# Other release and set points for loads and turns in a gated attention unit followed by an expert layer; one buffer moved from the gate tiles to the score tiles

## The chip, the cores and the metric

The kernel runs on one core of one Trainium2 chip. The metric is the device time of one execution in microseconds. Each version was run several times, in rounds with the kernel before on the same chip. Runs within 1.5% of the fastest of the same kernel count as fast, and only those are compared. A ratio is the mean time of one kernel's fast runs over that of the other's of the same rounds, so it is not quite the ratio of the medians quoted beside it.

## The reference

Per batch of 8, with 3008 rows: z is 64 wide, u and v are 256 wide.

```python
scores = (1 / S) * z @ z.T
attn   = maximum(scores, 0) ** 2
x      = u * (attn @ v)              # 24064 rows in all
h      = x @ w_in                    # 256 -> 2048
out    = (h * cos(h)) @ w_out        # 2048 -> 256
```

## The kernel before

A batch is cut into 6 chunks of 512 columns; a chunk is 8 steps of the schedule, a batch 48. `at(t, rank, f)` puts the emission of `f` at step t; all events are sorted by t and then emitted, so a set point largely decides the order of instructions on each engine. The scores are symmetric: a group (c, R) of four 128x512 score tiles is computed once and its mirror image is made by a DMA transpose, here called a turn. All turns stand on one queue, that of SyncE, nearly in the order of emission; the orders told below are read from the traces. Plain loads with a cast are issued by GpSimd (POOL in the profile).

```python
    def hold(dma):                       # a DMA waits for the last matmul emitted before it
        if before:
            after(dma.ins, before[-1], SYNC)

    def turn_z(b):                       # next batch's z, 13 + 12 blocks of 128x128
        for k in range(2):
            hold(nc.sync.dma_start_transpose(zT[b % 2][...], zst[...]))

    def s_diagonal(b, c, also):          # half of group (c, c), completed by three small turns
        ...
    def s_group(b, c, R, also=None):
        if R == c and not direct(b, c, R):
            return s_diagonal(b, c, also)
        ...                              # scores, relu (ACT), square (DVE) into tile `a`
        if R > c and not direct(b, R, c):
            nc.sync.dma_start_transpose(tt, t)        # the score turn

    for b in range(B):                   # t = 48 * b
        ...
            at(t - 3.5 * U, 0, lambda b=b: load_z(b))       # step -28 of the next batch
            at(t - 2.25 * U, 0, lambda b=b: turn_z(b))      # step -18
            for g in range(NG):                             # v loads at -20, -14, -8
                at(t + (0.75 * g - 2.5) * U, 0, lambda b=b, g=g: load_v(b, g))
        # (cuts; the first score group of a batch stands at step -13.1,
        #  groups (4,5) and (5,5) of the batch before at -18.1 and -17.1)
```

## Time and profile before

The median was 1270.74 us in the first rounds. The page's first part (share of the span in which each engine is busy) and its row of the granted TensorE clock (40 equal slices, tenths of full speed). PE is TensorE, PEld its weight loads, DVE VectorE, ACT ScalarE, POOL GpSimd, and SPq below is the queue of SyncE:

```profile
span 1270.7 us, 20219 instructions
PE 1249.6 (98%) x7533; PEld 673.1 (53%) x7533; DVE 787.8 (62%) x1302; ACT 854.4 (67%) x1516; POOL 145.8 (11%) x201
...
PEclk9989999999999999999999999999999999999999
```

TensorE bounds the kernel. The table of windows, one line per batch period (length, busy time of each engine, clock, DMA share, GB/s), shows that a batch in the middle has no idle TensorE at all:

```profile
207.56:363.53 155.97, 155.97 (x950) 84.77 (x948) 97.36 (x163) 107.67 (x192) 17.91 (x24) 1.00 0.74 118
```

Most of what is lost, about 17 of 21 us, is lost in the first 85 us. The list of waits of TensorE (total us, times, longest us), where `x` is VectorE's gating of a finished chunk and `a<-a` are the three turns of a diagonal group:

```profile
PE acc L308 <- DVE x L324: 7.9, 3, 5.4
PE acc L308 <- DMA a<-a: 2.4, 1, 2.4
...
PE acc L308 <- DMA v_0_65<-in_v_dram: 1.0, 1, 1.0
```

The timeline of SyncE's queue says why the gate of chunk 2 came 5.4 us late: its u turn stood behind five score turns that took 30.9 us.

```profile
34.92 30.91 SPq L268 DMA_TRANSPOSE tt<-a  x5
66.00 1.81 SPq L149 DMA_TRANSPOSE ut<-ust_61  x1
```

And the timeline around the end of a batch. Second column: duration; for the queue this is the time to issue, not to land.

```profile
250.76 4.57 SPq L112 DMA_TRANSPOSE zT_63<-zst  x2
...
255.43 3.65 SPq L268 DMA_TRANSPOSE tt<-a  x1
259.19 3.75 SPq L233 DMA_TRANSPOSE a<-a  x3
...
263.96 0.89 POOL L89 DMA_DIRECT2D v_1_66<-in_v_dram  x1 [10.38 <-PE w L338]
...
265.92 0.45 PE L218 MATMUL w<-zT_63 64*128 64x512 f16 x4
```

The next batch's z turns are issued at 250.8 us and used at 265.9 us, 15 us later.

### The profile page before, as it was taken

How to read it: one execution, taken by the hardware profiler on the slowest of the kernel's cores; microseconds unless marked ns; L12 is line 12 of the kernel's file. 1: busy time of each engine (PE TensorE's matmuls, PEld its weight loads, DVE VectorE, ACT ScalarE, POOL GpSimd, SP SyncE). 2: the span in 40 equal slices, each digit the busy share in tenths (PEclk: the TensorE clock that was granted, in tenths of full speed). 3: DMA queues.
4: the chain of work that ended last, by engine and by line, in shares of the span. 5: the costliest groups of instructions: out<-in, count | busy, mean ns of one | idle time of the engine just before them, and what ended most of it. 6: DMA issues, size and time to landing. Idle time of an engine off the chain costs nothing.

```text
span 1270.7 us, 20219 instructions
## 1 busy us (share of the span) xinstructions
PE 1249.6 (98%) x7533; PEld 673.1 (53%) x7533; DVE 787.8 (62%) x1302; ACT 854.4 (67%) x1516; POOL 145.8 (11%) x201
## 2 busy tenths in 40 slices
PE   8879999999999999999999999999999999999998
PEld 3335555555555555555555555555555555555556
DVE  6746666666666666665666666665666666665555
ACT  5646776666767666676667666766677666676646
POOL 3201101110011100211002110011100111000000
PEclk9989999999999999999999999999999999999999
DMA  9988855887679775888568885688857798565311
GB/s 157 149 142 129 136 103 94 125 119 137 100 110 125 127 113 106 118 133 123 101 109 111 136 139 91 106 115 138 126 93 118 109 144 115 107 109 100 76 34 43
DMA packets 485042, 145.03 MB, mean 114 GB/s; under 512 B 433232, under 2 KB 484944, under 8 KB 484944
## 3 DMA queue, kind: packets, MB, share of 16 engines
q1 hardware_dynamic: 357312, 88.92, 41.9%
q0 software_dynamic: 100400, 29.77, 24.3%
q10 hardware_dynamic: 27232, 25.06, 6.9%
q8 instruction: 59, 0.97, 0.3%
q14 instruction: 39, 0.32, 0.1%
HBM read 60.29 MB, written 24.64 MB: 67 GB/s over the span
## 4 chain that ended last, share of the span: by engine, by line
PE 96%; DMA 3%; DVE 1%; ACT 0%; SPq 0%; issue 0%; DVEq 0%
PE acc L308 36%; PE yp L362 26%; PE w L338 25%; PE w L248 5%; PE w L218 1%; DMA tt<-a 1%; DMA ut<-ust_62 1%; PE acc L281 1%; PE w L362 1%; DMA v_0_65<-in_v_dram 1%; DMA a<-a 0%; DMA ut<-ust_61 0%; PE w L453 0%; DVE g L345 0%; DVE x L324 0%; SPq L268 0%
## 5 line engine op out<-in xcount | busy, mean ns | idle before, releaser
L338 PE MATMUL w<-x,w_in_72 128*128 128x512 f16 x1504 | 447.0, 380 | 0.6 <-DVE g L345 0.3
L362 PE MATMUL yp<-w_out_73,g 128*128 128x256 f16 x2944 | 442.4, 273 | 0.4 <-ACT ob L370 0.4
L362 PEld LDWEIGHTS <-g 128*128 128x128 f16 x3008 | 285.2, 98 | 207.4 <-issue 41.5
L260 ACT ACTIVATE rt<-w 128x512 f16<-128x512 f32 x485 | 250.8, 602 | 110.9 <-PE w L248 110.9
L263 DVE TENSOR_TENSOR a<-rt 128x1024 f16<-128x1024 f16 x252 | 172.5, 690 | 158.9 <-ACT rt L260 156.0
L338 PEld LDWEIGHTS <-w_in_72 128*128 128x128 f16 x1504 | 147.2, 98 | 22.9 <-issue 4.2
L89 POOL DMA_DIRECT2D ust_62<-in_u_dram x64 | 45.2, 711 | 369.4 <-PE w L248 361.9
L228 ACT ACTIVATE rt<-w 128x512 f16<-128x512 f32 (+3 forms) x180 | 64.1, 442 | 32.6 <-PE w L218 32.6
L308 PE MATMUL acc<-a,v_2_70 128*128 128x512 f16 x304 | 76.1, 379 | 0.0
L308 PE MATMUL acc<-a,v_2_67 128*128 128x512 f16 x304 | 75.8, 379 | 0.0
L89 POOL DMA_DIRECT2D ust_61<-in_u_dram x48 | 36.1, 758 | 317.0 <-PE acc L308 304.5
L308 PE MATMUL acc<-tt,v_0_68 128*128 128x512 f16 (+1 forms) x288 | 70.3, 373 | 0.0
L324 DVE TENSOR_TENSOR x<-acc,ut 128x128 f16<-128x128 f32 (+7 forms) x89 | 62.5, 713 | 9.4 <-DMA ut<-ust_61 5.9
L229 DVE TENSOR_TENSOR a<-rt 128x512 f16<-128x512 f16 (+3 forms) x180 | 49.3, 323 | 30.6 <-ACT rt L228 27.8
L308 PE MATMUL acc<-a,v_1_66 128*128 128x512 f16 x224 | 57.7, 387 | 9.5 <-DVE x L324 7.1
L308 PEld LDWEIGHTS <-v_1_66 128*128 128x128 f16 x384 | 36.7, 98 | 57.3 <-issue 17.2
L308 PE MATMUL acc<-tt,v_0_65 128*128 128x512 f16 (+1 forms) x264 | 64.3, 373 | 0.0
L308 PEld LDWEIGHTS <-v_0_65 128*128 128x128 f16 x384 | 36.8, 98 | 50.0 <-issue 7.6
L308 PEld LDWEIGHTS <-v_0_68 128*128 128x128 f16 x384 | 36.9, 98 | 45.8 <-issue 3.4
L308 PEld LDWEIGHTS <-v_1_69 128*128 128x128 f16 x384 | 36.9, 98 | 45.0 <-issue 2.6
L370 ACT ACTIVATE ob<-yp 128x512 f32<-128x512 f32 x92 | 55.8, 607 | 1.2 <-PE yp L362 1.2
L308 PE MATMUL acc<-a,v_1_69 128*128 128x512 f16 x224 | 56.2, 379 | 0.0
(1557 smaller groups left out, 1501.2 us busy)
## 6 DMA issues: line engine op xcount, KB each, us to landing
out_dram<-ob ACTq DMA_DIRECT2D x94, 256.0 KB, 3.1
ust_61<-in_u_dram POOLq DMA_DIRECT2D x48, 128.0 KB, 5.8
ust_62<-in_u_dram POOLq DMA_DIRECT2D x32, 128.0 KB, 3.4
a<-a SPq DMA_TRANSPOSE x135, 2.9
v_0_65<-in_v_dram POOLq DMA_DIRECT2D x4, 512.0 KB, 6.7
v_1_66<-in_v_dram POOLq DMA_DIRECT2D x4, 512.0 KB, 7.1
v_0_68<-in_v_dram POOLq DMA_DIRECT2D x4, 512.0 KB, 7.3
v_1_69<-in_v_dram POOLq DMA_DIRECT2D x4, 512.0 KB, 6.5
```

The costliest lines, as they stand in the source:

```text
L89: hold(nc.gpsimd.dma_start(dst, src))
L218: chain(nc.tensor.matmul(sps[k][:, k * P:], zt[h, j0 + k, :], zt[h, j0 + k:j0 + K, :].rearrange("p j w -> p (j w)"), start=True, stop=True))
L228: nc.scalar.activation(rt[:, i, k * P:], sps[k][:, k * P:], AF.Relu)
L229: nc.vector.tensor_tensor(t[:, k, k:, :].rearrange("p s w -> p (s w)"), rt[:, i, k * P:], rt[:, i, k * P:], ALU.mult)
L248: chain(nc.tensor.matmul(sps[k], zt[h, R * K + k + 1 - lo, :], zt[h, j0:j0 + K, :].rearrange("p j w -> p (j w)"), start=True, stop=True))
L260: nc.scalar.activation(rt[:, i, :], sps[k0 + i], AF.Relu)
L263: nc.vector.tensor_tensor(tv, rv, rv, ALU.mult)
L308: chain(nc.tensor.matmul(acc[:, nh, 0:wn], vt[:, j % G, nh * P:(nh + 1) * P], a, start=(n == 0), stop=(n == NJ - 2)))
L324: nc.vector.tensor_tensor(xs[m][:, :, at:at + n], acc[:, :, o:o + n], ut[:, :, o:o + n], ALU.mult)
L338: chain(nc.tensor.matmul(hp, w_in16[:, k, ft * P:(ft + 1) * P], x[:, k, :], start=(k == 0), stop=(k == NDH - 1)))
L362: chain(nc.tensor.matmul(ys[m][:, ts % YP, :], gs[(m, ft // FG)][:, ft % FG, ts * P:(ts + 1) * P], w_out16[:, ft, :], start=(n % (YP * NFT ...
L370: nc.scalar.activation(ob, ys[m], AF.Copy, bias=0.0, scale=inv_s2)
```

## The change

It tries to shorten the start (loads released earlier, the u turn of chunk 2 earlier on the queue, no turns for group (0,3,3), more `a` buffers), and to move the next batch's z load and z turns later.

```diff
-        if before:
-            after(dma.ins, before[-1], SYNC)
+        after(dma.ins, gate[0] if gate else before[-1], SYNC)   # gate: 5th of 8 warm-up matmuls
...
-    gpool = pool("g", 7)
+    gpool = pool("g", 6)
-    apool = pool("a", 8)
+    apool = pool("a", 9)
...
-        if R == c and not direct(b, c, R):
+        if R == c and (b, c) > (0, 3):          # (0,3,3) becomes a full group
...
-                at(12 + 3 * q, 0, lambda q=q: load_w_out(q))
+                at(15 + 2 * q, 0, lambda q=q: load_w_out(q))
...
-            at(t - 3.5 * U, 0, lambda b=b: load_z(b))
-            at(t - 2.25 * U, 0, lambda b=b: turn_z(b))
+            at(t - 2.75 * U, 0, lambda b=b: load_z(b))       # step -22
+            at(t - 2.125 * U, 0, lambda b=b: turn_z(b))      # step -17
...
-            at(t + c * U + (1 if c != 1 or b else -3), 0, lambda b=b, c=c: turn_u(b, c))
+            at(t + c * U + (1 if b or c not in (1, 2) else -3 * c), 0, lambda b=b, c=c: turn_u(b, c))
```

Between steps -18 and -17 stands the score group (5,5). The turn of (4,5), emitted at -18.1, stands in the trace before the change just behind the z turns of -18 (at 255.43 us). So on SyncE's queue the z turns fall from before the score turn of (4,5) to behind that turn and behind the three turns of (5,5).

More of the change, by code (lines that the diff above doesn't have):

```diff
@@ L81, in chain @@
         before.append(mm.ins)
+    gate = []
     def hold(dma):
-        if before:
-            after(dma.ins, before[-1], SYNC)
+        after(dma.ins, gate[0] if gate else before[-1], SYNC)
     def load(dst, src):
@@ L430 @@
                 at(-80 + i, 0, f)
+            at(-70, 0, gate.clear)
             at(2, 0, lambda: load_u(0, 2))
@@ L454, in prepare @@
                 wp, zero[:, 0, 0:P], zero[:, 0, :], start=True, stop=True))
+            if i == 4:
+                gate.append(before[-1])
         make_identity(nc, ident)
```

## The prediction

> **What bounds it.** TensorE is busy 98% of 1270.7 us (page, part 1); the table of windows by batch shows it busy 155.97 of 155.97 us in batches 1 to 6, so nothing is to be won there. The loss, about 21 us of idle TensorE in all, is mostly in the first 85 us.
>
> Waits of TensorE (list of waits; timeline of PE):
> - 0.97 us at 11.6 us for the first v load, issued at 5.14 us when the 8th warm-up matmul ended.
> - 1.78 us at 45 us for VectorE's gate of chunk 1, whose turned u landed at 43.88 us.
> - 1.31 + 0.33 + 0.23 + 0.22 us between 56 and 63 us, while VectorE waited 2.84 us for an `a` buffer whose turn landed at 59.88 us.
> - 5.37 us until 71.3 us for the gate of chunk 2: its turned u stood behind five score turns (30.9 us on SyncE's queue) and landed at 69.9 us.
> - 2.39 us at 74.7 us for the three turns that complete the diagonal group (0,3,3).
> - The granted clock is 0.50 from 70 to 80 us; TensorE is busy 6.1 us there, so this costs about 3 us (estimate). The Trainium skill, "TensorE: Matmul & The Clock Gate", Part 1, says an idle TensorE drops to half clock, by windows of about 3.4 us; the trace agrees: dips of about 3.4 us (from 12) and 10 us.
>
> **What the change does.**
> - The turn of u chunk 2 now follows one score turn of the second run, not five: issue near 41 us, landing near 50, needed near 63. The 5.37 us go.
> - (0,3,3) becomes a full group: the 2.39 us wait goes; TensorE pays 0.60 instead of about 0.44 us.
> - Without these gaps the clock should stay up: 3 us. Together about -10.5.
> - The ninth `a` buffer and the later next-batch z load (issued at 52.9 us, into saturated DMA) relieve VectorE's 2.84 us wait: -0.7. The inserted u turn delays score turns by about 3 us, which takes part back.
> - Release by the fifth warm-up matmul (0.45 us each) issues the first loads 1.35 us earlier: -1.0, and perhaps part of the dip at 12 us (-0.3 on average).
> - Chunk 1's turned u, somewhat earlier: -0.4.
> - Six g buffers: by the schedule a buffer is free two steps (about 6 us) before reuse: 0.
> - Danger: the turns of the next batch's z move behind the score turn of (4,5) and the diagonal turns of (5,5). In batch 1 they start at 250.8 us and are needed at 265.9. I expect a start near 259.5 and landing near 265 (estimate: 3.75 us for three diagonal turns, 5.5 for both z turns). That may stall 0 to 1 us, seven times: about +1.5.
>
> Sum: 1270.7 - 10.5 - 0.7 - 1.3 - 0.4 + 0.2 + 1.5 = 1259.5 us.
>
> **What would show it.** Waits of PE: none for DVE x over 1.5 us, none for a<-a; clock 1.00 from 60 to 85 us; first v load issued near 3.8 us, chunk 0 starting near 10.6 us, chunk 3 near 62 to 64 us instead of 71.3; batches still 155.97 us apart (if z stalls: score matmuls waiting on the z turn, 156 to 157).
>
> **What would make it wrong.** Delayed score turns hold the `a` buffers, VectorE stalls at 55 to 62 us and gives several us back; a dip of the clock survives; or the z turns stall every batch by over 1 us (up to +8). The other way: the early clock dip vanishes too (-1.5).
>
> Over 2% needs 25 us, more than all idle time.

## The result

| | median us | runs | range us |
|---|---|---|---|
| before | 1270.55 | 6 | 1265.65 to 1271.01 |
| changed | 1312.04 | 6 | 1302.11 to 1314.60 |

The ratio is 1.0328, with a 95% interval of 1.0291 to 1.0365: slower, where 1259.5 was predicted. The page of the changed kernel shows where the clock fell, in four slices of its row. Two more dips show only in the windows: one at 1078 us, which falls across two slices (0.93 from 1050 to 1100 us), and a shorter one at 918 us, just after a wait of 1.83 us on a z turn (0.97 in the last line, one of the table of windows):

```profile
span 1309.0 us, 20210 instructions
PE 1260.1 (96%) x7533; PEld 676.8 (52%) x7533; DVE 789.2 (60%) x1300; ACT 855.5 (65%) x1516; POOL 145.6 (11%) x201
...
PEclk9998999989999999998999989999999999999999
...
900.00:950.00 50.00, 48.16 (x287) 26.14 (x286) 29.07 (x49) 32.34 (x59) 7.10 (x10) 0.97 0.86 127
```

The waits of TensorE name the cause. The gate of chunk 2 and the diagonal turns are gone, as predicted; in their place score matmuls wait for the z turns, seven times, once for each next batch:

```profile
PE w L219 <- DMA zT_64<-zst: 21.2, 4, 7.3
PE w L219 <- DMA zT_63<-zst: 16.5, 3, 7.5
PE acc L309 <- DVE x L325: 1.8, 2, 1.0
```

The same stretch as above, in the timeline of the changed kernel:

```profile
258.60 3.96 SPq L113 DMA_TRANSPOSE zT_63<-zst  x2
...
260.65 0.89 POOL L90 DMA_DIRECT2D v_1_66<-in_v_dram  x1 [9.42 <-PE acc L309]
...
270.93 0.71 PE L219 MATMUL w<-zT_63 64*128 64x512 f16 x4 [7.55 <-DMA zT_63<-zst]
```

The turns are issued 7.8 us later than before on the clock, and 10.4 us later relative to the work, since this kernel was some 2.5 us ahead at this point. Their own wait (`hold`) took at most 0.03 us, so it is the queue ahead of them that sets their start. They then need 12.3 us from first issue to use, as the v load comes right behind them. The windows of 5 us show the price, first of idle TensorE and then of half clock (second number: busy TensorE; third from the end: clock):

```profile
260.00:265.00 5.00, 3.38 (x20) 1.74 (x18) 2.08 (x3) 1.38 (x2) 0.89 (x1) 1.00 1.03 169
265.00:270.00 5.00, 0.00 (x0) 0.00 (x0) 0.00 (x0) 0.00 (x0) 0.00 (x0) 0.61 1.42 138
270.00:275.00 5.00, 4.07 (x18) 2.07 (x19) 1.43 (x5) 2.11 (x5) 0.00 (x0) 0.50 0.40 79
275.00:280.00 5.00, 5.00 (x26) 2.53 (x24) 1.89 (x4) 2.06 (x3) 0.00 (x0) 0.86 0.10 20
```

The clock is down for about 10 us. During 5.5 us of it TensorE works, at half speed, and loses about 2.7 us (an estimate from these windows). By windows of 1 us, the dips of batches 1, 2, 4, 5 and 7 lost 1.7, 2.7, 2.0, 1.8 and 1.6 us in the same way, 9.8 in all; the dip of batch 6, from 918.1 to 921.5 us, lost another 1.7, so 11.5.

The seven batches are not alike. This table was put together from the timeline and from the landing times of the z turns:

| next batch | 2nd z turn issued | v load issued | lead us | 2nd turn landed after us | TensorE waited us |
|---|---|---|---|---|---|
| 1 | 94.7 | 95.92 | 1.2 | 11.0 | 7.09 |
| 2 | 260.1 | 260.65 | 0.5 | 10.8 | 7.55 |
| 3 | 424.8 | 426.86 | 2.1 | 5.4 | 0.58 |
| 4 | 583.0 | 583.48 | 0.5 | 10.2 | 7.07 |
| 5 | 747.1 | 748.47 | 1.4 | 10.4 | 6.30 |
| 6 | 910.9 | 912.50 | 1.6 | 6.1 | 1.83 |
| 7 | 1071.6 | 1072.06 | 0.5 | 10.5 | 7.28 |

In this one trace a lead of 1.6 us or more landed in about 6 us, a lead of 1.4 us or less in over 10 (e2 and e10 below show that 1.6 us is no general limit). That made the theory. Queue Q1: the later place on SyncE's queue alone costs the time. Queue and collision Q2: the late turns also meet the v load, and most of the loss is that. Rivals: the z load at step -22 arrives too late (L), or the buffers or other parts cost it (P).

### The profile page after: what moved, and what is told of

Same layout as the page of the kernel before. It is cut to its first block, busy times and chain, and to the rows that moved or that the text cites. A ratio compares the mean times of both kernels' runs of the same rounds, so it can differ in the third digit from the quotient of the medians.

```text
span 1309.0 us, 20210 instructions
## 1 busy us (share of the span) xinstructions
PE 1260.1 (96%) x7533; PEld 676.8 (52%) x7533; DVE 789.2 (60%) x1300; ACT 855.5 (65%) x1516; POOL 145.6 (11%) x201
## 4 chain that ended last, share of the span: by engine, by line
PE 92%; DMA 6%; ACT 1%; DVE 1%; issue 0%; SPq 0%; DVEq 0%; ACTq 0%
PE acc L309 34%; PE yp L363 25%; PE w L339 24%; PE w L249 5%; DMA zT_64<-zst 3%; DMA zT_63<-zst 2%; PE w L219 1%; PE acc L282 1%; DMA ut<-ust_62 1%; PE w L363 1%; DVE g L346 0%; DVE x L325 0%; DMA x<-in_z_dram 0%; SPq L113 0%; PE w L192 0%
## 5 line engine op out<-in xcount | busy, mean ns | idle before, releaser
L363 PE MATMUL yp<-w_out_73,g 128*128 128x256 f16 x2944 | 446.9, 275 | 0.4 <-ACT ob L371 0.4
```

What stands on the lines that cost most here:

```text
L363: chain(nc.tensor.matmul(ys[m][:, ts % YP, :], gs[(m, ft // FG)][:, ft % FG, ts * P:(ts + 1) * P], w_out16[:, ft, :], start=(n % (YP * NFT ...
```

## The experiments

Twelve runs of ten kernels (e11 is e1 again, e12 is e8 again), all correct. e1 to e4 ran on one chip, the others on another.

**e1_zturn_back: undo the set point of the z turns alone.**

```diff
-            at(t - 2.125 * U, 0, lambda b=b: turn_z(b))
+            at(t - 2.25 * U, 0, lambda b=b: turn_z(b))
```

> The changed kernel with one part undone: the turns of the next batch's z at step -18 again instead of -17. Theory Q (the later set point puts these turns behind other turns on SyncE's queue and into the v load): the seven waits of score matmuls on the z turns go, each worth 5.4 us idle on average and about 1.7 us of half clock, so about 1312 - 7 x 7.1 = 1262 us; only the early gain of about 11 us against the kernel before is left: 1258 to 1262. Rival L (the z load, now at step -22, arrives too late for the turns): the wait stays or gets worse, 1305 or more. Rival P (fewer g buffers, or the other parts, cost the time): stays near 1312.

Measured: 1258.29, 1258.38 and 1263.65 us, ratio to the kernel before 0.9937 (0.9891 to 0.9983). One run, the profiled one (1387.3 us, clock 0.88), is left out. The whole loss hangs on this one set point; the z load at -22, the buffers and the rest lose nothing that shows. Rivals L and P fall. The same kernel was timed again below as e11. (The 1261 us in later expectations is a median that counts the slow run; the fast runs have a mean of 1260.1.)

**e2_only_zturn: the kernel before with this set point alone** (-18 to -17, nothing else).

> The kernel before with only the z turns at step -17. Theory Q: the whole loss and nothing of the gain: 1270.5 + 35 to 55 us, so 1305 to 1325, with waits of score matmuls on the z turns in the profile, up to 7.5 us each. Rivals L and P: 1270.

Measured: 1297.18 us, ratio 1.0243 (1.0181 to 1.0305). Sufficient too, but smaller than I expected: its profile has seven waits on z turns of 21.9 us in all, the longest 5.9.

```profile
PE w L218 <- DMA zT<-zst: 21.9, 7, 5.9
```

The clock fell in three of the batches only (three windows of 50 us with 0.93). In these three the v load was issued 1.2 to 1.7 us after the second turn, which landed after 9.1 to 9.5 us, and TensorE waited 5.5 to 5.9 us. In the other four the lead was 2.1 to 2.3 us, the turn landed in 5.3 to 5.6 us, and the wait was 1.1 to 1.3 us. Why the leads were longer here was not looked into.

**e3_only_zload: the kernel before with only the z load later** (-28 to -22).

> The kernel before with only the next batch's z load at step -22 instead of -28. Theory Q: no loss; 1270, or up to 3 us less, since the first of these loads leaves the crowded stretch before 65 us. Rival L: waits on the z turns, 1290 or more.

Measured: 1262.09 us, ratio 0.9952 (0.9908 to 0.9995). No loss, and a gain of about 6 us, twice what I allowed. Its profile has no 5.4 us wait for the gate of chunk 2 any more, though the u turn of chunk 2 stands where it stood, behind five score turns. These now took 23.2 us instead of 30.9:

```profile
31.63 23.21 SPq L268 DMA_TRANSPOSE tt<-a  x5
55.00 1.25 SPq L149 DMA_TRANSPOSE ut<-ust  x1
```

In the kernel before, the load of the next batch's z was issued from 52.9 us on and had landed by 65.8 us. The last two of the five turns fell into that stretch and took 12.3 us to issue, against 6.9 us here: 5.4 of the 7.7 us. So this load had slowed the turns behind it. The first three, issued before it, took 18.5 us against 16.2; that part is not explained by it. From 60 to 65 us the DMA engines moved 159 GB/s, at a DMA share of 1.60, so this stretch was crowded.

**e4_v1_later: the changed kernel, z turns still at -17, the colliding v load at -12 instead of -14.**

```diff
-                at(t + (0.75 * g - 2.5) * U, 0, lambda b=b, g=g: load_v(b, g))
+                at(t + (-20, -12, -8)[g], 0, lambda b=b, g=g: load_v(b, g))
```

> The changed kernel, z turns still at step -17, but the second v load of each next batch at step -12 instead of -14, so after the first score matmuls that wait. Theory Q2 (the late place on the queue alone costs 0 to 2 us; the rest comes from the second z turn sharing the DMA engines with the 512 KB v load issued about 1 us after it): the second z turn lands 4 to 6.5 us after its issue in all batches, as it did in batches 3 and 6, waits of 0 to 2 us and no dip of the clock there: 1260 to 1272. Theory Q1 (the place on the queue alone): landing stays at 10 to 11 us, 1305 to 1315.

Measured: 1275.45 us, 36.6 less than the changed kernel's median (other rounds). The z turns keep their late place, yet land within 4.0 to 7.4 us, and the clock stays at 1.00 in every batch. The wait left over is this:

```profile
PE w L219 <- DMA zT<-zst: 13.1, 7, 3.3
```

This separates the two shares. Against e11's profile without such waits (span 1257.4 us, below), this one is 1270.1 us long: 12.7 us for the place on the queue, which agrees with the 13.1 us of waits. The changed kernel's span is 1309.0 us, 38.9 more. Of these about 3 belong to its start (TensorE came up to full speed later in that execution: chunk 1 began at 30.11 us, here at 27.13); the other 36 went with the v load. They are longer waits on the z turns (37.7 - 13.1 = 24.6 us) and the half clock behind them (11.5 us), and they agree with the medians. I had given the place 0 to 2 us a batch, and it took 1.9 on average; the total came out 3 us above my range. Q1 falls, Q2 stands.

**e5_zturn_17_2: the z turns between the two set points.**

```diff
-            at(t - 2.125 * U, 0, lambda b=b: turn_z(b))
+            at(t - 2.15 * U, 0, lambda b=b: turn_z(b))
```

> The changed kernel with the z turns at step -17.2 in place of -17: on SyncE's queue still behind the score turn of (4,5), but ahead of the three diagonal turns of (5,5). They should be issued 3 to 4 us earlier, so that the second one is out at least 3 us before the v load. If the lead over the v load decides (in the changed kernel a lead of 1.6 and 2.1 us landed in 6 us, one of 1.4 us or less in over 10), they land 5 to 7 us after issue and score matmuls do not wait: 1257 to 1264 us, as with -18. If any turn later than step -18 is too late, waits of 2 us and more stay: over 1275.

Measured: 1259.44 us, no wait on a z turn, landing in 3.8 to 6.0 us. In the batch shown above they are issued at 243.81 us and used at 253.24, with the three diagonal turns (3.77 us to issue) now behind them. Those three small turns decide between no loss and some 50 us.

**e10_v1_early: collision without lateness.** The kernel of e1 with the v load right behind the z turns.

```diff
-                at(t + (0.75 * g - 2.5) * U, 0, lambda b=b, g=g: load_v(b, g))
+                at(t + (-20, -17.3, -8)[g], 0, lambda b=b, g=g: load_v(b, g))
```

> The kernel with z turns at step -18, and the second v load of each next batch moved from step -14 to -17.3, right behind these turns, so that the two collide on the DMA engines while the turns still stand early on SyncE's queue. If the loss needs both (a late place and a collision), some z turns take 9 us or more to land, but score matmuls do not wait, as there are some 15 us from issue to use: 1257 to 1264. If the collision alone costs time: 1275 or more.

Measured: 1259.01 us and no wait on a z turn, although five of the seven second turns landed only after 8.9 to 10.3 us (the line has the first turns too):

```profile
DMA to landing us min/median/max: 5.6/6.6/10.3
```

The collision costs nothing where there is slack. The late place alone costs 12.7 us (e4); the larger part of the loss, 36 us, needs both. And the lead does not decide alone: here six of the leads were 1.75 to 2.0 us, and four of those turns took 8.9 to 10.3 us, two 6.4 and 6.8. What decides below a lead of about 2 us was not found.

**The parts of the start**, each undone in the kernel of e1:

**e6_uturn_back: the u turn of chunk 2 back behind five score turns.** The edit restores the old `turn_u` line.

> The kernel with z turns at step -18 (1261 us), and the turn of u chunk 2 back at its old place behind five score turns. Theory U (the prediction: that place on the queue cost the 5.4 us wait and about 2 us of clock): 1266 to 1270, with a wait of 3 us or more for VectorE's gate of chunk 2 in the profile. Theory Z (the z load in the crowded stretch slowed that queue; the run with only this load moved was 8 us faster and had no such wait): within 1.5 us of 1261 and no such wait.

Measured: 1263.86 us, 5.2 more than the base on the same chip (e11, 1258.64, other rounds). The longest wait for a gate, that of chunk 2, is 2.2 us:

```profile
PE acc L309 <- DVE x L325: 3.7, 3, 2.2
```

Behind it the clock fell for 3.4 us, which lost about 1.7 us (estimate). It falls between the two theories: the new place is worth about 2 us of wait and this dip once the z load is out of the way, not 5.4 us of wait.

**e7_diag_back: group (0,3,3) diagonal again.** The edit restores the old condition.

> The kernel with z turns at step -18 (1261 us), and the group (0,3,3) diagonal again, with its three turns. If these turns cost what the prediction said, a wait of 2.4 us or more for them stays in the profile at the start of chunk 3, and some half clock: 1263 to 1268. If the relieved queue now hides them: 1261.

Measured: 1265.43 us (1260.67 to 1271.88), and the wait is there, longer than before the change:

```profile
PE acc L309 <- DMA a<-a: 5.4, 2, 5.2
```

The half clock behind it lost about 1.5 us more (estimate). The median is 6.8 us above e11's. The three turns do cost what the prediction said and more; making the group full is a gain.

**e8_gate_8: first loads released by the eighth warm-up matmul again** (`if i == 7`).

> The kernel with z turns at step -18 (1261 us), and the first loads released by the eighth warm-up matmul again. The prediction gave the fifth 1.0 us and a share of the early dip. By the profiles of two runs without an early dip, chunk 1 started at 27.13 us with the fifth and at 27.67 us with the eighth: so 0.5 us, 1261.5, too little for the total to show; the profile should show a wait of 0.6 to 1.0 us for the first v load.

Measured: 1259.05 us. The wait for the first v load was 0.2 us, not 0.6 to 1.0, and the total is no worse. Timed again as e12, beside e11.

**e9_pools_back: 7 g and 8 a buffers.**

> The kernel with z turns at step -18 (1261 us), with 7 g and 8 a buffers as before. The prediction gave the ninth a buffer and the relieved DMA together 0.7 us and the g buffer nothing. Since the score turns now land earlier, a wait of VectorE for an a buffer of at most 1 us: 1258 to 1262, not to be told from 1261 by the total; the profile should show at most 0.5 us of new waits of TensorE.

Measured: 1261.32 us, two runs at 1258.3 and two at 1264.3 and 1265.3; the profile, of a run of 1258.3 us, has no wait of TensorE over 0.3 us that e11's lacks. No gain from the exchange of buffers shows there; the two longer runs have no profile, so what made them longer stays open.

**e11_zturn18_gate5 and e12_zturn18_gate8: five rounds each, side by side.**

> The same kernel as e1_zturn_back (z turns at step -18, first loads released by the fifth warm-up matmul), for a profile in the fast state and to be set against the next one: 1258 to 1263, no waits on z turns; chunk 3 starts at 61 to 65 us.

> The same kernel as e8_gate_8 (the best of those run so far), timed again beside the one with the fifth. If the earlier release is worth the 1.0 us of the prediction, this one is 1.0 slower; by the last runs (1259.05 against 1261.0, other rounds) I expect it equal or up to 1.5 us faster: 1258 to 1262, and faster than the kernel before by 0.3 to 0.8%.

| | median us | range us | ratio to before | 95% interval |
|---|---|---|---|---|
| e11, fifth | 1258.64 | 1257.87 to 1260.29 | 0.9943 | 0.9902 to 0.9983 |
| e12, eighth | 1260.20 | 1259.01 to 1260.72 | 0.9953 | 0.9917 to 0.9989 |
| before | 1265.82 | 1260.84 to 1273.02 | | |

e11 is the better one here by 1.6 us; in the earlier runs, on different chips, the fast ones had means of 1260.1 (e1, fifth) and 1259.4 us (e8, eighth). The gate is not settled beyond "within 2 us". e11, the change without its z turn set point, beats both kernels, the one before by 0.6%: clear of the noise. Its page and its only notable waits:

```profile
span 1257.4 us, 20210 instructions
PE 1246.0 (99%) x7533; PEld 672.4 (53%) x7533; DVE 788.9 (63%) x1300; ACT 854.1 (68%) x1516; POOL 145.5 (12%) x201
...
PEclk9999999999999999999999999999999999999999
```

```profile
PE acc L309 <- DVE x L325: 1.6, 2, 0.8
PE w L249 <- DVE g L346: 1.4, 2, 1.2
```

The account closes: the changed kernel's span is 51.6 us longer than this one (1309.0 - 1257.4). It has 37.7 us of waits on z turns, about 11.5 us lost in six dips of the clock, and its profiled execution was 2.4 us later into chunk 3 (64.93 against 62.52 us): 51.6 us (estimate).

Why the earlier release gains so little is visible in the timelines. In e11 GpSimd issues the first v load at 3.86 us and VectorE's casts of z run into it; in e12 they don't, and take 0.43 us:

```profile
3.86 1.02 POOL L90 DMA_DIRECT2D v<-in_v_dram  x1 [2.55 <-PE w L455]
4.36 0.75 DVE L187 CAST zst<-x 128x512 f16<-128x512 f32 x1 [2.96 <-DMA x<-in_z_dram]
```

```profile
4.03 0.43 DVE L187 CAST zst<-x 128x512 f16<-128x512 f32 x1 [2.63 <-DMA x<-in_z_dram]
...
5.14 1.07 POOL L90 DMA_DIRECT2D v<-in_v_dram  x1 [3.83 <-PE w L455]
```

The first score matmuls started at 7.30 us in e11 and at 6.78 us in e12; the first chunk at 11.71 and 11.42 us. What the v load gains, the z path loses. The Trainium skill, "SBUF — State Buffer", § Who interferes with whom, says that a cast on VectorE can take a pair of ports that it shares with GpSimd, and that the one that comes second then waits. The longer cast agrees with it (0.75 against 0.43 us), but not every cast beside such an issue was longer (in e12 one at 5.30 us took 0.43), so this stays a possible cause, not shown.

## Why the prediction was wrong

- **What bounds the kernel, and that the batches hold no gain:** right. That they could hold a loss was seen, but mis-sized.
- **The step that failed** is the last one: "That may stall 0 to 1 us, seven times: about +1.5." The mechanism, the z turns behind the turns of (4,5) and (5,5), was right, and so was nearly the start: 259.5 us expected, which with this kernel's 2.5 us lead would be 257.0, and 258.60 measured. The landing was wrong: 5.5 us for both turns. In the trace of the kernel before, a single z turn landed 5.4 to 7.4 us after its own issue, and the pair 7.2 to 9.0 us after the first issue. From 259.5 us that alone gives waits of about 1 to 3 us for a use at 265.9 (estimate), and e4 measured 1.9 us on average. Without the v load beside them the turns took about 7 us from first issue to use (e4: issued at 247.96, used at 254.85 us), and with the v load on the engines 12.3. The waits were 5.4 us on average and up to 7.5 (37.7 in all), not 0 to 1.
- **What was not asked:** what else starts at that time. The v load at 263.96 us stood in the trace, 2 us before the use of the turns. The Trainium skill, "DMA: Bandwidth & Descriptors", § Issuing engines are not separate DMA queues, says that DMAs from several issuing engines run "on the same 16 DMA engines and interleave with each other"; the landing of 10.2 to 11.0 instead of 5.4 to 6.1 us agrees. About 36 of the 50 us went with this load (e4). I had treated SyncE's queue as the only thing in the way.
- **What was left out:** the clock. The skill's page "TensorE: Matmul & The Clock Gate", Part 1, was used for the dips of the start, but not applied to the danger. The five waits of 6.3 us and more each brought a dip that cost 1.6 to 2.7 us, and so did the wait of 1.83 us (1.7 us); the wait of 0.58 us brought none, nor did those of e4, up to 3.3 us. So for waits of 1.3 to 3.3 us their length does not tell whether a dip follows, and what does was not found.
- **The gain of the start:** the direction was right, and the waits named went. The size was read from one profile. That profile fell in one of the longer executions of the kernel before (1272.7 us); its runs spread from 1260.8 to 1273.0 us, so the gain on the mean is 7 us (0.9943), not the 12.7 that the listed terms sum to. Why the kernel before spreads so, and e11 (1257.9 to 1260.3) does not, was not tested; its shortest run had a mean clock of 0.999 and its longest one of 0.995, which is about 5 of the 12 us (estimate).
- **Its parts:** the 5.4 us wait for chunk 2 was put down to the place on the queue. e3 removed it without touching that place, by taking the z load out of the crowded stretch; the place is worth 2.2 us of wait and about 1.7 us of half clock beside that (e6). The diagonal turns were sized too low (5.4 us of waits in e7 against 2.4). For the gate (1.0 us plus 0.3) and the `a` buffer no gain shows (e8, e9, e12).

## What to carry to other kernels

When a transfer moves later, look up when its reader needs it, what is queued ahead of it and which other transfers are released in between, on any queue; size its landing by the crowded case, not by the shortest one in the trace. A small loss that repeats in every period outweighs a gain in a start-up: here 50 us lost against 7 gained on the mean. And a wait behind a queue can be cured by emptying the engines under it as well as by reordering it.

## What the Trainium skill lacked or had wrong

- "DMA: Bandwidth & Descriptors": it says that queues interleave, but not how sharply this can show for a DMA transpose. Here the second of two turns (12 blocks of 128x128) landed in 9.1 to 11.0 us when a 512 KB load on another queue was issued 0.5 to 1.4 us after it (changed kernel and e2), in 5.3 to 9.3 us when it was 1.6 to 2.3 us (changed kernel and e2; up to 10.3 us in e10), and in 3.8 to 5.4 us when it was 4.7 us or more (e5).
- "DMA: Bandwidth & Descriptors": no figure for what a cast-load of narrow rows does to turns in flight. Two score turns took 12.3 us to issue with the 64-wide z load beside them, and 6.9 without (the last two of the five in e3).
- "TensorE: Matmul & The Clock Gate", § HAM oscillation: its advice to avoid idle gaps over about 3.4 us agrees with these runs, since each of the eleven waits of 4.4 us and more in four traces brought half clock. But shorter gaps are not safe: waits of 1.3 us (e2), 1.8 (changed kernel), 2.2 (e6) and 2.9 (e3) were followed by 3.4 us of half clock too, while six waits of 1.3 to 3.3 us in e4 were not. A dip cost 1.5 to 2.7 us beside the wait itself (an estimate from the traces).
